# A linear-attention and SOLU feed-forward kernel on one core: the low mantissa bits of its weights made by another instruction on another engine, some copies moved to GpSimd, and a new order list

## The chip, the core and the metric

The kernel runs on one core of a Trainium2 chip. Five engines work side by side: TensorE (PE, with its weight loads shown apart as PEld), VectorE (DVE), ScalarE (ACT), GpSimd (POOL) and SyncE (SP), which issues all of this kernel's DMAs. Each engine takes its own instructions strictly in order. The metric is the device time of one execution in microseconds; the number compared is the median of several runs.

## What is computed

Eight batches, eight heads, 576 positions, head dimension 64. Linear attention gives 4608 rows of 512, and a feed-forward layer with a SOLU activation and a layer norm follows:

```python
q_s = softmax(q, axis=-1); k_s = softmax(k, axis=2)
kv = np.einsum('bhsd,bhse->bhde', k_s, v)
x = np.einsum('bhsd,bhde->bhse', q_s, kv)   # then turned to 4608 x 512
h = x @ w_in                                # 512 x 1024
solu = h * softmax(h)
ln = (solu - mean) / np.sqrt(var + 1e-06) * g_ln
return ln @ w_out                           # 1024 x 512
```

q, k, v and g_ln come as 4-byte floats. [...]

## The kernel before

The 4608 rows are 36 row tiles of 128. Works have short names: `K<b>` is the keys of batch b (column maxima, exponentials, the product with v, its scaled halves `bd`), `Q<b>a`, `Q<b>b`, `Q<b>c` and `R<b>` the queries, `V<b><i>` the load of a quarter of v and its copy into `vm` beside a column of ones, `x<t>` the attention product of row tiles from t on, `h<t>` the first matrix product of row tile t with everything up to the transposed activations `uT`, `o<t>` the second product and the store. `w<i>` and `y<i>` load and convert a quarter of w_in and of w_out, `W` and `Z` cut the converted weights into two half-precision parts `wi` and `wo` (part 0 is the value rounded to half precision, the "high half"; part 1 is the rest, the "low half"), and `P` is four products on zeros whose result nobody reads.

Every work is a generator. `ORDER` is a list, written out by hand, of steps: `step` advances the named work to its next yield, and a suffix `.v` sets `chosen`, so that `on(default)` returns VectorE in that step and the default engine otherwise. So the list fixes the order of the instructions on every engine, and no scheduler changes it.

**Converting the weights.** `float_of` (lines 251 to 264) takes a tile of words and makes the floats in three steps: ACT multiplies the high word, read as a float, into place (L259), DVE shifts the result's bits left by three (L261), and DVE shifts the low word right by 29 and puts its top three bits in (L263). Eight tiles of 128x1024 go through it, four `iw` and four `gw`. The words lie in a pool of two buffers, so the load of a tile waits until the words of the tile two before have been read. ACT then sums the absolute values of each converted tile (L276, L313); from the sums, by way of a product on PE (`wide_in`, `wide_out`), come the scales `s_in` and `s_out`, and from these `wi` (L288 on ACT, L290 on DVE, four tiles) and `wo` (L335 on ACT, L337 on DVE, eight pieces of 128x512).

**The first four row tiles.** They do not wait for `wi`: they multiply with `iw` itself at full 4-byte precision (L612, blocks in the order 3, 0, 2, 1). Their hidden values h lie in two PSUM buffers, so h of tile 2 starts when tile 0 has been read for the last time. In a tile the chain is: maximum on DVE (L627), its negative `nm` on ACT (L629), exponentials on ACT (L633), four small steps `am`, `pi`, `p`, `ph` on POOL or DVE (L637 to L646), the product on DVE (L649), the mean `nmu` on ACT (L651), `u` on ACT (L654), its rest on DVE (L656), the squares on ACT (L663). All later tiles multiply the half-precision parts (L620). The second product (L694) needs `wo` and `uT`.

The change and the prediction touch `float_of`, `load_v` (L212), `weights_in_scaled` (L288), `weights_out_scaled` (L335) and the list. In the changed kernel the code behind `float_of` stands eight lines lower (L620 is L628 there, L694 is L702).

## Time and profile before

| what | value |
|---|---|
| median of 3 runs | 464.75 us (463.77 to 465.03) |
| the profiled execution, its own time | 464.6 us |
| its span, first to last instruction | 462.8 us |
| PE busy | 439.2 us, 95% of the span |
| DVE, ACT, POOL busy | 339.3, 285.2, 202.6 us |
| mean granted TensorE clock | 0.999 |

The profiled execution's own time is 1.8 us longer than its span, and 0.15 us under the median. A busy PE is not a PE at its peak: durations of matmuls are modelled, and neighbours in a row overlap in the record, so that the start of the next row tells more than the duration. Idle time of PE is the quantity to follow.

### The profile page before, as it was taken

Reading aid. Unit: us, or ns where it says so; the run is one execution under the profiler, and the core shown is the slowest. Engines: PE = TensorE matmul, PEld = TensorE weight load, DVE = VectorE, ACT = ScalarE, POOL = GpSimd, SP = SyncE. Lnnn points to the kernel's source line nnn. Section 1 sums busy time; section 2 is a strip of 40 time slices with the busy share of each in tenths; the row PEclk is TensorE's granted clock in tenths of the full one; section 3 lists DMA queues with packets and bytes.
Section 4 is the critical chain, followed back from the end, with each engine's and each line's share of the span. In section 5 each row is a group of like instructions: output and inputs, shape, how many; then the busy total and the mean of one; then the engine's idle time right before and its main releaser. Section 6 shows DMA issues by size and latency. Waiting matters only on the chain.

```text
span 462.8 us, 8794 instructions
## 1 busy us (share of the span) xinstructions
PE 439.2 (95%) x3379; PEld 212.9 (46%) x3379; DVE 339.3 (73%) x622; ACT 285.2 (62%) x492; POOL 202.6 (44%) x308
## 2 busy tenths in 40 slices
PE   0688999999999999999999999999999999999997
PEld 0344444455445445444544445444454444444445
DVE  4989999987987979986987888675778553541711
ACT  2779998777767768385756674567635654441500
POOL 2112856487776664741455575126613421122010
PEclk9999999999999999999999999999999999999999
DMA  8897866788698496958697857774342562322252
GB/s 280 292 305 267 239 137 184 149 226 203 179 230 187 89 243 111 273 114 217 120 252 153 180 121 185 203 166 86 86 93 68 92 130 77 72 66 68 59 120 72
DMA packets 137386, 73.98 MB, mean 160 GB/s; under 512 B 114168, under 2 KB 122624, under 8 KB 137344
## 3 DMA queue, kind: packets, MB, share of 16 engines
q1 hardware_dynamic: 137344, 73.42, 65.1%
q8 instruction: 26, 0.43, 0.4%
q14 instruction: 16, 0.13, 0.1%
HBM read 36.70 MB, written 9.44 MB: 100 GB/s over the span
## 4 chain that ended last, share of the span: by engine, by line
PE 86%; ACT 7%; DVE 3%; DMA 1%; issue 1%; SPq 0%; ACTq 0%
PE o L694 41%; PE h L620 36%; PE kv L397 4%; PE x L585 3%; DMA km<-in_k_dram 1%; ACT gw L259 1%; ACT e L633 1%; PE h L612 1%; ACT km L385 1%; ACT wi L288 1%; ACT junk_out L313 1%; PE warm_up L751 1%; PE wide L358 1%; DVE iw L263 1%; ACT e L663 1%
## 5 line engine op out<-in xcount | busy, mean ns | idle before, releaser
L694 PE MATMUL o<-wo,uT 128*128 128x512 f16 (+1 forms) x888 | 197.8, 373 | 0.0
L620 PE MATMUL h<-wi,xT 128*128 128x512 f16 x768 | 178.0, 379 | 0.3 <-ACT e L663 0.3
L694 PEld LDWEIGHTS <-uT 128*128 128x128 f16 x888 | 85.8, 98 | 97.7 <-issue 1.6
L620 PEld LDWEIGHTS <-xT 128*128 128x128 f16 x768 | 74.3, 98 | 88.2 <-issue 1.8
L627 DVE TENSOR_REDUCE top<-h 128x1 f32<-128x1024 f32 x36 | 44.0, 1221 | 29.3 <-PE h L620 29.1
L656 DVE SCALAR_TENSOR_TENSOR u<-h,nmu,u 128x1024 f16<-128x1024 f32 x36 | 45.8, 1275 | 16.3 <-ACT u L654 16.1
L663 ACT ACTIVATE e<-h,nmu 128x1024 f32<-128x1024 f32 x36 | 40.1, 1113 | 21.2 <-DVE u L656 21.1
L649 DVE SCALAR_TENSOR_TENSOR h<-h,ph,e 128x1024 f32<-128x1024 f32 x36 | 46.1, 1283 | 8.1 <-POOL ph L646 6.1
L637 POOL TENSOR_SCALAR am<-nm 128x1 f32<-128x1 f32 x20 | 9.1, 454 | 80.7 <-ACT nm L629 80.6
L643 POOL TENSOR_TENSOR p<-pi,mone 128x1 f32<-128x1 f32 x36 | 25.5, 708 | 39.9 <-DVE pi L640 38.4
L654 ACT ACTIVATE u<-h,nmu 128x1024 f16<-128x1024 f32 x36 | 40.0, 1113 | 1.0
L633 ACT ACTIVATE e<-h,nm,hs 128x1024 f32<-128x1024 f32 x28 | 33.7, 1202 | 0.7
L704 ACT ACTIVATE os<-o,rr 128x512 f32<-128x512 f32 (+1 forms) x21 | 14.2, 674 | 30.2 <-PE o L694 22.9
L651 ACT ACTIVATE nmu<-s 128x1 f32<-128x1 f32 x36 | 7.3, 202 | 39.8 <-DVE h L649 31.9
L449 POOL TENSOR_TENSOR qm<-qm,qnmx 128x1024 f32<-128x1024 f32 (+1 forms) x12 | 21.1, 1770 | 20.6 <-DVE qnmx L447 20.5
L612 PE MATMUL h<-iw,xT 128*128 128x512 f32 x64 | 29.5, 599 | 0.1
L629 ACT ACTIVATE nm<-top,hs 128x1 f32<-128x1 f32 x28 | 8.2, 294 | 33.4 <-DVE top L627 33.4
L467 POOL TENSOR_TENSOR qm<-qm,qrec 128x1024 f32<-128x1024 f32 x12 | 23.0, 1920 | 11.7 <-DVE qrec L458 5.4
L383 POOL TENSOR_TENSOR km<-km,kb 128x1152 f32<-128x1152 f32 x10 | 26.3, 2632 | 3.4 <-ACT kb L361 3.2
L597 DVE SCALAR_TENSOR_TENSOR xT<-x,xT 128x512 f16<-128x512 f32 (+1 forms) x36 | 22.3, 623 | 7.2 <-ACT xT L595 7.1
L702 DVE TENSOR_SCALAR os<-o,rr 128x512 f32<-128x512 f32 (+1 forms) x16 | 11.6, 728 | 20.6 <-PE o L694 15.3
L474 POOL TENSOR_TENSOR qhl<-qm,qhl 128x512 f16<-128x512 f32 x20 | 24.1, 1228 | 5.3 <-ACT qhl L160 5.1
(147 smaller groups left out, 559.9 us busy)
## 6 DMA issues: line engine op xcount, KB each, us to landing
v<-in_v_dram SPq DMA_DIRECT2D x32, 288.0 KB, 3.9
km<-in_k_dram SPq DMA_DIRECT2D x7, 1152.0 KB, 6.4
out_dram<-os SPq DMA_DIRECT2D x31, 256.0 KB, 2.7
qm<-in_q_dram SPq DMA_DIRECT2D x7, 1024.0 KB, 6.7
w_in<-in_moe_w_in_dram SPq DMA_DIRECT2D x8, 512.0 KB, 8.4
w_out<-in_moe_w_out_dram SPq DMA_DIRECT2D x8, 512.0 KB, 5.8
out_dram<-os SPq DMA_DIRECT2D x10, 128.0 KB, 2.3
km<-in_k_dram SPq DMA_DIRECT2D x2, 576.0 KB, 6.8
```

Source lines behind the costliest of these rows:

```text
L383: on(nc.gpsimd).tensor_tensor(km[:, ns], km[:, ns], wide, op=ALU.subtract)
L474: on(nc.gpsimd).tensor_tensor(lo, y, hi, op=ALU.subtract)
L612: nc.tensor.matmul(h[:, ns], xT[:, kc], iw[kc][:, ns], start=(i == 0), stop=(i == NP - 1))
L620: nc.tensor.matmul(h[:, ns], xT[:, t, kc], wi[:, s, kc, ns], start=(i == 0), stop=(i == len(terms) - 1))
L627: nc.vector.tensor_reduce(top, h, axis=AX.X, op=ALU.max, negate=True)
L633: nc.scalar.activation(e, h, AF.Exp, bias=nm, scale=hs, accum_out=z)
L643: nc.gpsimd.tensor_tensor(p, pi, mone, op=ALU.pow)
L649: nc.vector.scalar_tensor_tensor(h, h, ph, e, op0=ALU.mult, op1=ALU.mult, accum_out=s1)
L654: nc.scalar.activation(u[:, 0], h, AF.Identity, bias=nmu)
L656: nc.vector.scalar_tensor_tensor(u[:, 1], h, nmu, u[:, 0], op0=ALU.add, op1=ALU.subtract)
L663: nc.scalar.activation(e, h, AF.Square, bias=nmu, accum_out=s2)
L694: nc.tensor.matmul(o, uT[:, j, f], wo[:, s, f, cols], start=(f == 0 and j == 0 and s == 0), stop=(f == NF - 1 and j == 1))
```

## The change

- `float_of` gets a step ahead of ACT's, which leaves the three bits as a small integer in the low word's place. In a step with `.v` DVE makes it (shift right by 29, a word in and a word out). In a step without, GpSimd makes it: it reads the low word's top byte as an unsigned 8-bit number, multiplies by 1/32, adds -31/64 and writes the rounded integer. What follows on DVE is one pass: shift the float's bits left by three and put the integer in. The pass that only shifted is gone.
- A new helper `scalar_or_pool` returns GpSimd in a step with `.v` and ACT otherwise. The copies of v use it in place of `on(nc.scalar)` (so `.v` there now means GpSimd, no longer DVE), and so do the high halves `wi` and `wo`, which were on ACT alone.
- `ORDER` is another list of the same works. It has nine `P` in place of eight.

```diff
+    def scalar_or_pool():
+        return nc.gpsimd if on(nc.scalar) is nc.vector else nc.scalar
...
-        cast(on(nc.scalar), vm[:, i, :, 0:D], t)
+        cast(scalar_or_pool(), vm[:, i, :, 0:D], t)
...
+        eng = on(nc.gpsimd)
+        if eng is nc.vector:
+            eng.tensor_scalar(low, low, 29, -1, op0=ALU.logical_shift_right, op1=ALU.bitwise_and)
+        else:
+            top = words.bitcast(U8)[:, :, 3]
+            eng.tensor_scalar(low, top, 1.0 / 32, -31.0 / 64, op0=ALU.mult, op1=ALU.add)
+        yield
         nc.scalar.activation(x, high.bitcast(F32), AF.Prelu, scale=2.0**-112, alpha=-(2.0**32))
         yield
-        nc.vector.tensor_scalar(xi, xi, 3, -1, op0=ALU.logical_shift_left, op1=ALU.bitwise_and)
-        yield
-        nc.vector.scalar_tensor_tensor(xi, low, 29, xi, op0=ALU.logical_shift_right, op1=ALU.bitwise_or)
+        nc.vector.scalar_tensor_tensor(xi, xi, 3, low, op0=ALU.logical_shift_left, op1=ALU.bitwise_or)
...
-            nc.scalar.activation(wi[:, 0, kc], iw[kc], AF.Copy, scale=s)
+            cast_scaled(scalar_or_pool(), wi[:, 0, kc], iw[kc], s)
...
-            nc.scalar.activation(wo[:, 0, f], x, AF.Copy, scale=g)
+            cast_scaled(scalar_or_pool(), wo[:, 0, f], x, g)
...
-    "LQ0*2 LK0 Q0a*2 Q0c LK0 K0.v Q0c.v K0 w3 K0.v K0 Q0b Q0a.v w3 K0 V02 Q0a Q0b K0.v Q0a.v Q0c V00 K0.v "
+    "LQ0*2 LK0*2 Q0a.v w3 Q0b.v Q0a Q0c V02.v P w3.v Q0b K0 K0.v Q0a K0*2 K0.v K0*2 V02.v Q0a V00.v w0.v "
```

Of the eight integer passes four are on DVE (`w_in` 3, 0, 1 and `w_out` 3) and four on POOL. Of the eight v copies of batches 0 and 1 seven are on POOL. Of the `wi` high halves one is on POOL, of the `wo` high halves two. Names in the order rows: the number behind a name tells one buffer from the next; `khalf`, `ktop` are the running maxima of the keys, `qm` and `km` the queries and keys of a batch, `qnmx`, `qsum`, `qden`, `qrec` the maxima and sums of the queries' softmax.

DVE at the start of the program, before:

```order
L449 TENSOR_TENSOR qm_95<-qm_95,qnmx_2_105 128x8x128
L374 TENSOR_TENSOR khalf_109<-khalf_109 128x2x128
L376 TENSOR_TENSOR ktop_108<-khalf_109 128x2x64
L377 TENSOR_TENSOR ktop_108<-ktop_108,km_98 128x2x64
L372 TENSOR_TENSOR khalf_109<-km_98 128x2x256
L447 TENSOR_REDUCE qnmx_1_118<-qm_95 128x8
L374 TENSOR_TENSOR khalf_109<-khalf_109 128x2x128
L454 TENSOR_REDUCE qsum_0_125<-qm_95 128x8
L456 TENSOR_SCALAR qden_0_127<-qsum_0_125 128x8
L458 RECIPROCAL qrec_0_129<-qden_0_127 128x8
L376 TENSOR_TENSOR ktop_108<-khalf_109 128x2x64
L377 TENSOR_TENSOR ktop_108<-ktop_108,km_98 128x2x64
```

and after:

```order
L455 TENSOR_REDUCE qnmx_2_110<-qm_95 128x16
L380 TENSOR_TENSOR khalf_122<-km_98 128x2x256
L382 TENSOR_TENSOR khalf_122<-khalf_122 128x2x128
L384 TENSOR_TENSOR ktop_121<-khalf_122 128x2x64
L385 TENSOR_TENSOR ktop_121<-ktop_121,km_98 128x2x64
L380 TENSOR_TENSOR khalf_122<-km_98 128x2x256
L382 TENSOR_TENSOR khalf_122<-khalf_122 128x2x128
L384 TENSOR_TENSOR ktop_121<-khalf_122 128x2x64
L385 TENSOR_TENSOR ktop_121<-ktop_121,km_98 128x2x64
L462 TENSOR_REDUCE qsum_0_136<-qm_95 128x8
L464 TENSOR_SCALAR qden_0_138<-qsum_0_136 128x8
L466 RECIPROCAL qrec_0_140<-qden_0_138 128x8
```

The key maxima `ktop` of batch 0 now stand together, ahead of the sums `qsum`; the addition into `qm` on DVE has gone further down. The first product on PE that needs data, the transpose of `ktop`, is released by the last of them.

POOL around the small steps of row tile 0 (`am`, `p`, `ph`), before:

```order
L464 TENSOR_TENSOR qn_2_104<-qm_95,qrec_2_289 128x2x4x64
L637 TENSOR_SCALAR am_0_450<-nm_0_431 128x1
L640 TENSOR_SCALAR pi_0_470<-am_0_450 128x1
L643 TENSOR_TENSOR p_0_473<-pi_0_470,mone 128x1
L646 TENSOR_TENSOR ph_0_475<-p_0_473,one 128x1
L383 TENSOR_TENSOR km_325<-km_325,kb_483 128x2x576
```

and after:

```order
L267 TENSOR_SCALAR w_in_205<-w_in_205 128x1024
L472 TENSOR_TENSOR qn_2_109<-qm_95,qrec_2_340 128x2x4x64
L267 TENSOR_SCALAR w_out_378<-w_out_378 128x1024
L168 COPY vm<-v_0_223 128x9x64
L645 TENSOR_SCALAR am_0_452<-nm_0_426 128x1
L267 TENSOR_SCALAR w_out_387<-w_out_387 128x1024
L651 TENSOR_TENSOR p_0_477<-pi_0_456,mone 128x1
L654 TENSOR_TENSOR ph_0_483<-p_0_477,one 128x1
L391 TENSOR_TENSOR km_347<-km_347,kb_490 128x2x576
```

Two integer passes on words of w_out and a copy of v now stand ahead of `ph`, on which row tile 0's product on DVE waits.

ACT around the exponentials `e` of row tile 0, before:

```order
L288 ACTIVATE wi<-iw_182,s_in 128x1024
L288 ACTIVATE wi<-iw_347,s_in 128x1024
L259 ACTIVATE gw_425<-w_out_397 128x1024
L426 ACTIVATE bd_80<-kvn_296,s_kv_358 64x256
L160 COPY vm<-v_2_395 128x9x64
L629 ACTIVATE nm_0_431<-top_0_429,one 128x1
L288 ACTIVATE wi<-iw_275,s_in 128x1024
L428 COPY bd_80<-bd_80 64x256
L259 ACTIVATE gw_445<-w_out_416 128x1024
L633 ACTIVATE e_0_447,z_0_448<-h_0_351,nm_0_431,one 128x1024
```

and after:

```order
L269 ACTIVATE gw_390<-w_out_378 128x1024
L637 ACTIVATE nm_0_426<-top_0_424,one 128x1
L641 ACTIVATE e_0_438,z_0_439<-h_0_370,nm_0_426,one 128x1024
L269 ACTIVATE gw_454<-w_out_387 128x1024
L172 ACTIVATE wi<-iw_202,s_in 128x1024
L434 ACTIVATE bd_80<-kvn_320,s_kv_368 64x256
L172 ACTIVATE xT_2_488<-x_2_0_465 128x256
L369 COPY kb_490<-wide_485 128x256
L436 COPY bd_80<-bd_80 64x256
L172 ACTIVATE wi<-iw_373,s_in 128x1024
```

The exponentials stood behind three high halves `wi`; now one conversion stands ahead of them and the first high half comes behind. A high half of the third block is no longer on ACT, and that of the last block comes only behind all `wo`, some forty rows further down.

## Rows read from the trace of the kernel before

**Rows 1.** The page's parts 1 and 2: busy time with share of the span and instruction count of each engine, then the busy tenths of 40 slices of 11.6 us.

```profile
PE 439.2 (95%) x3379; PEld 212.9 (46%) x3379; DVE 339.3 (73%) x622; ACT 285.2 (62%) x492; POOL 202.6 (44%) x308
...
DVE  4989999987987979986987888675778553541711
ACT  2779998777767768385756674567635654441500
POOL 2112856487776664741455575126613421122010
```

**Rows 2.** The windows view of core 0 for the stretch before 72.5 us and the stretch behind it; columns: stretch, its length, busy time (and instructions) of PE, PEld, DVE, ACT, POOL, granted TensorE clock as a share of full speed, DMA share, GB/s.

```profile
0.00:72.50 72.50, 52.34 (x493) 26.49 (x494) 62.25 (x120) 57.99 (x96) 26.01 (x33) 1.00 0.79 244
72.50:463.00 390.50, 386.90 (x2886) 186.41 (x2885) 277.08 (x503) 227.25 (x397) 176.56 (x276) 1.00 0.63 144
```

**Rows 3.** The waits view of PE over the whole span; columns: who waited for whom, us in total, times, longest.

```profile
PE turned L348 <- DVE ktop L377: 14.3, 1, 14.3
PE wide L358 <- ACT cols L160: 2.2, 2, 1.5
PE kv L397 <- ACT km L385: 1.1, 1, 1.1
...
PE h L620 <- ACT e L663: 0.3, 1, 0.3
```

**Rows 4.** The timeline of PE from 0 to 120 us; columns: start, duration (both us), engine, line, operation, out<-in, shape, count, and in brackets the idle time before it with its releaser.

```profile
14.29 0.66 PE L348 MATMUL turned<-ident,ktop 128*128 128x128 f32 x2 [14.29 <-DVE ktop L377]
...
17.23 1.91 PE L751 MATMUL warm_up<-bd 128*128 128x512 f16 x4
...
22.38 1.89 PE L751 MATMUL warm_up<-bd 128*128 128x512 f16 x4
24.19 1.58 PE L397 MATMUL kv<-vm,km 64*64 64x65 f32 x72
...
26.20 1.03 PE L751 MATMUL warm_up<-bd 128*128 128x512 f16 x4
...
34.30 3.60 PE L612 MATMUL h<-iw,xT 128*128 128x512 f32 x8
...
51.25 7.03 PE L612 MATMUL h<-iw,xT 128*128 128x512 f32 x16
...
72.53 1.89 PE L620 MATMUL h<-wi,xT 128*128 128x512 f16 x8 [0.27 <-ACT e L663]
74.25 1.46 PE L694 MATMUL o<-wo,uT 128*128 128x512 f16 x6
```

**Rows 5.** The timeline of DVE from 0 to 90 us, same columns.

```profile
8.76 1.22 DVE L449 TENSOR_TENSOR qm<-qm,qnmx 128x1024 f32<-128x1024 f32 x1
...
12.41 0.68 DVE L454 TENSOR_REDUCE qsum<-qm 128x8 f32<-128x512 f32 x1
...
13.85 0.29 DVE L377 TENSOR_TENSOR ktop<-ktop,km 128x128 f32<-128x128 f32 x1
...
26.70 1.39 DVE L261 TENSOR_SCALAR iw<-iw 128x1024 int32<-128x1024 int32 x1
...
31.43 1.23 DVE L263 SCALAR_TENSOR_TENSOR iw<-w_in,iw 128x1024 int32<-128x1024 int32 x1
...
38.17 1.22 DVE L627 TENSOR_REDUCE top<-h 128x1 f32<-128x1024 f32 x1
...
45.73 1.29 DVE L649 SCALAR_TENSOR_TENSOR h<-h,ph,e 128x1024 f32<-128x1024 f32 x1
...
68.71 0.23 DVE L330 TENSOR_SCALAR gs<-gl,s_out 128x8 f32<-128x8 f32 x1
```

**Rows 6.** The timeline of ACT from 0 to 90 us, same columns.

```profile
40.16 0.29 ACT L629 ACTIVATE nm<-top,one 128x1 f32<-128x1 f32 x1
...
43.00 1.19 ACT L633 ACTIVATE e<-h,nm,one 128x1024 f32<-128x1024 f32 x1
...
49.87 1.11 ACT L663 ACTIVATE e<-h,nmu 128x1024 f32<-128x1024 f32 x1
...
65.20 1.08 ACT L313 ACTIVATE junk_out<-gw 128x1024 f32<-128x1024 f32 x1
...
71.28 1.10 ACT L663 ACTIVATE e<-h,nmu 128x1024 f32<-128x1024 f32 x1
```

**Rows 7.** Groups of DVE instructions by line, shapes kept apart, over the whole span; columns: line, engine, operation, out<-in, shapes, count, busy us, mean ns of one, idle before.

```profile
L263 DVE SCALAR_TENSOR_TENSOR gw<-w_out,gw 128x1024 int32<-128x1024 int32 x4 | 4.9, 1222 | 0.0
...
L261 DVE TENSOR_SCALAR gw<-gw 128x1024 int32<-128x1024 int32 x4 | 2.7, 684 | 0.0
```

**Rows 8.** Groups of ACT instructions by line, shapes kept apart, of the stretch 0 to 72.5 us, same columns.

```profile
L160 ACT COPY vm<-v 128x576 f32<-128x576 f32 x8 | 5.3, 668 | 0.0
...
L288 ACT ACTIVATE wi<-iw,s_in 128x1024 f16<-128x1024 f32 x4 | 4.5, 1138 | 0.0
```

**Rows 9.** Groups of POOL instructions by line, shapes kept apart, over the whole span, same columns.

```profile
L449 POOL TENSOR_TENSOR qm<-qm,qnmx 128x1024 f32<-128x1024 f32 x10 | 18.9, 1904 | 11.6 <-DVE qnmx L447 11.5
...
L449 POOL TENSOR_TENSOR qm<-qm,qnmx 128x512 f32<-128x512 f32 x2 | 2.2, 1098 | 9.0 <-DVE qnmx L447 9.0
...
L143 POOL MEMSET bd<- 128x1024 f16 x1 | 1.0, 952 | 0.3 <-POOLq L800 0.3
```

**Rows 10.** The timeline of POOL from 0 to 120 us, columns as in the other timelines.

```profile
26.49 1.05 POOL L464 TENSOR_TENSOR qn<-qm,qrec 128x512 f32<-128x512 f32 x1 [2.52 <-PE qt L519]
```

More of the change, by code (lines that the diff above doesn't have):

```diff
@@ L13 @@
 I32 = mybir.dt.int32
+U8 = mybir.dt.uint8
 AF = mybir.ActivationFunctionType
```

145 rows, old and new, of the table ORDER are left out of this document.

## The prediction

> **What bounds the kernel now.** I read the busy shares first, then where PE is idle, then the chain that ends PE's idle time. PE is busy for 95% of the span, DVE, the next, for 73% [rows 1]. So the question is what PE's idle time is made of. The windows say that it lies at the two ends: up to 72.5 us PE is busy for 52.3 us, so 20.2 are idle, and in the 390.5 behind that only 3.6 are [rows 2]. Of these 3.6 a wait of 0.3 is the only one; the rest follows the last product. The waits of PE agree: 14.3 us until the first transpose of the keys' maxima, some small ones, and 0.3 for the squares of a row tile [rows 3], which is the wait in front of the row at 72.53 [rows 4]. From there on PE works without a gap.
>
> So the kernel's time is a start plus a constant: 72.53, then 390.3 to the end of the span (462.8), then 1.8 outside the span, 464.6 for the profiled execution; the median of the runs is 464.75. The work of PE behind 72.53 is the same in both kernels (the same products, and the warm-ups all lie ahead), so whatever the change does off PE there costs nothing as long as PE does not run dry. What can move the time is the start.
>
> In the start DVE is busy for 62.3 us of 72.5 and ACT for 58.0, POOL for 26.0 [rows 2]; from the third to the seventh slice DVE is at 8 or 9 tenths or more and ACT at 7 to 9 [rows 1]. PE fills its time there with products whose result nobody reads. Two chains cross: weights (words, float, sum, scale, halves) and the first four row tiles, each of which passes DVE and ACT eight times and holds one of two PSUM buffers meanwhile.
>
> **What the change takes away and adds.** Up to the scales of w_out, ACT loses seven of eight v copies at 0.668 and two of four `wi` high halves at 1.138 [rows 8]: 4.7 + 2.3 = 7.0 us. DVE loses four of eight passes at 0.684 [rows 7], 2.7 us, and takes over half of the subtraction on batch 1's keys, 1152 elements, about 1.4 by L263's pace (1.222 for 1024 [rows 7]): net 1.3 less. Only half of the "second pass" really leaves DVE; the other half stays as a pass on the words. POOL gets four byte passes, seven copies, one high half. Nothing like them is in the trace, so they are bounded: for 1024 elements 0.95, the memset that only writes, to 1.90, the two-input sum; for 576 elements 0.54 to 1.24, by the same two rows and the 512-element one scaled [rows 9]. All together 8.5 to 18 us; POOL goes from 26 to some 35 to 44 of 72.5, so it is not full, but what stands behind a late piece waits. I take 1.3 for a byte pass, between the ends since it reads one stream and writes one. None of these can be below nothing: they are added instructions. The cost of the two `wo` high halves on POOL lies behind the scales, beside DVE's low halves.
>
> The DVE pass on words with a gap between them is not in the trace either: the same operation on dense data takes 0.684, a pass at one element a cycle 1.222 [rows 7]. I take 0.95, the middle; each then costs 0.27 over the dense one, 0.8 for the three on w_in; the fourth, on w_out, I take as hidden beside ACT's sums.
>
> The Trainium skill, "VectorE: DVE Perf Modes", section "What auto-detection actually checks", gives the double rate to one source and a destination in SBUF whose outermost dimension is even, as 1024 is, whatever the gap. By it the pass takes 0.684 and the time comes out 0.8 us lower, 461.6; no row here shows the gapped pass.
>
> **The path, checkpoint by checkpoint** (before, then after).
>
> 1. First transpose of the maxima: 14.29 [rows 4]. On DVE the 1.22 of the addition at 8.76 and the sums from 12.41 to the last maximum but one (13.85 less 12.41, less one 0.27 step, 1.2) stood between the maxima [rows 5]; both now come behind. 14.29 - 2.4 = 11.9, or 14.29 if the second part of the keys lands late; I take 12.3. Only part of this is carried on, since the exponentials of the keys also wait for DVE.
>
> 2. End of row tile 0's full-precision products: 34.30 + 3.60 = 37.9 [rows 4]. The last conversion they need ended at 31.43 + 1.23 = 32.7 [rows 5]. Off DVE ahead of it are now the pass of 1.39 at 26.70 (now POOL's) and the last block's own pass, which runs beside ACT's: 2.0 less, 30.6. Behind it one block, half of 3.60, and two transposes, and the wait for `wide_in` stands behind: 33.5. Gain 4.4.
>
> 3. Product of row tile 0 on DVE: 45.73 [rows 5]. The maximum (38.17 [rows 5]) comes behind batch 1's key maxima at 34.5, the exponentials then follow `nm` at once (before: 40.16 to 43.00 [rows 6], behind high halves). But DVE has two conversions, a low half (1.28, as the other two-source passes) and the scale chain to do in between: 34.5 + 1.2 + 1.2 + 1.2 + 1.3 and 2.1 of small steps = 41.5. Gain 4.2.
>
> 4. End of its squares, which frees the buffer for row tile 2: 49.87 + 1.11 = 51.0 [rows 6]. Now an exponential of the keys and that of row tile 1 (1.19) stand ahead of the squares: gain 3.1, 47.9; row tile 2's products on PE (51.25 before [rows 4]) follow at once.
>
> 5. Last sum of w_out: 65.20 + 1.08 = 66.3 [rows 6], and the scales 68.71 [rows 5]. Row tiles 1 and 2 carry the gain of the buffer on: 63.2 and 65.7.
>
> 6. Start of the gapless stretch: 72.53 [rows 4]. It now begins with the second product, which before came second at 74.25 [rows 4]. It needs two low halves of `wo` behind the scales and a rest of `u` on DVE, 65.7 + 0.2 + 1.3 + 1.5 = 68.7, and PE has the last blocks of row tile 3 to finish, 69.1. Raw gain 3.4.
>
> From this I take off 0.8 for the gapped DVE passes and 0.4 for two-source passes that meet a POOL instruction (below). 70.3 + 390.3 + 1.8 = **462.4 us**, 2.2 less than the profiled execution.
>
> TensorE's clock is granted at full (2.4 GHz) throughout in the record [rows 2], yet four warm-up products took 1.91 and 1.89 at first and 1.03 from 26.20 [rows 4]. The list now starts them ahead of the first transpose. At the slow pace the products on batch 0's keys end about where I have them, at the fast one 1 us earlier; since row tile 0 waits for its weights, I count nothing.
>
> **Rivals.** *DVE alone sets the start.* With DVE nearly full, ACT's 7 us are worth nothing and only DVE's own 1.3 less count, minus the 1.2 taken off: 464.5, with 463.4 to 465.2 around it. For it: the digits of DVE [rows 1]. Against it: the rows of ACT ahead of the exponentials (2.8 us from `nm` to `e`) are on the path.
>
> *POOL and DVE block each other*, the one that ends slower. The DVE pass at 26.70 took 1.39, where its like take 0.684 [rows 5, 7], and POOL's instruction from 26.49 to 27.54 lies over it [rows 10]: 0.7 us lost in one meeting. The change adds twelve POOL instructions ahead of the scales, and DVE has some twenty passes there with two operands in SBUF. Eight meetings would take 5.6 of a raw gain of 3.4: 466.8. From five on the gain is gone. A late byte pass does the same by another way, since `ph` stands behind two of them.
>
> The Trainium skill, "SBUF — State Buffer", section "Who interferes with whom", has this as a rule: a DVE instruction in a two-port mode, or one with two SBUF inputs against a GpSimd instruction that reads SBUF, and that instruction exclude each other for their whole length. By that rule this rival's price holds for every meeting; the trace agrees, 1.39 against 0.684. It leaves open how many meet.
>
> *PE runs dry later.* The last `wi` block's high half now comes behind all of `wo` on ACT, and its low half behind row tile 3's product on DVE. I work out its end at 79.5, and PE wants it 11.2 us into the gapless stretch, about 81. If the chain is 3 us late, PE waits 1.5 or more: 464.
>
> **How the numbers follow.** The forecast with its own range 460.4 to 463.3: 0.60. DVE alone: 0.22. PE dry later: 0.05. Blocking: 0.13. The range for 8 in 10 takes in all but the last and the edges: 459.9 (gapped passes at the double rate, no meeting, the clock 1 us earlier) to 465.2. A difference under 0.3%, 1.4 us, can't be told from none: faster 0.60 (the forecast), same 0.27 (DVE alone and PE dry, 463.4 to 466.1), slower 0.13 (blocking).
>
> **What would show it.** Right: PE's first transpose near 12.3, row tile 0's squares ending near 48, the scales near 66, the gapless stretch starting near 70.3 and no wait of PE behind it. DVE alone: the early checkpoints move, the scales stay above 68. Blocking: conversions on DVE (L271) well over 1.25 us in the mean. The forecast is wrong if a byte pass takes over 2 us, or if PE waits after 71.

## The result, and the profile after

The changed kernel is slower: 466.84 us in the median of 12 runs (465.54 to 468.91) against 464.45 us of 12 runs of the kernel before (463.77 to 465.89) on the same chip, a ratio of 1.0057 with a 95% interval of 1.0044 to 1.0071. The forecast was 462.4. Executions of the changed kernel lie up to 3.4 us apart, those of the kernel before 2.1; so a single profile is read below for order and for the length of single instructions, and times are compared by medians.

The profiled execution took 467.61 us, with a span of 465.8. TensorE (PE), its waits and its first and last steps of the start, as in [rows 4]:

```profile
12.45 0.66 PE L356 MATMUL turned<-ident,ktop 128*128 128x128 f32 x2 [8.84 <-DVE ktop L385]
...
33.29 3.60 PE L620 MATMUL h<-iw,xT 128*128 128x512 f32 x8
...
51.75 8.83 PE L620 MATMUL h<-iw,xT 128*128 128x512 f32 x16 [2.43 <-ACT e L671]
...
74.75 2.75 PE L702 MATMUL o<-wo,uT 128*128 128x512 f16 x12
```

The first transpose comes 1.84 us earlier than in [rows 4], as forecast. Of that, 1.0 is left when row tile 0's products end (33.29 + 3.60 = 36.9), and the gapless stretch starts 2.2 us later than before. VectorE (DVE) on the way, to be held against the same forms in [rows 5, 7]:

```profile
17.55 1.84 DVE L391 TENSOR_TENSOR km<-km,kb 128x1152 f32<-128x1152 f32 x1
...
20.38 1.34 DVE L391 TENSOR_TENSOR km<-km,kb 128x1152 f32<-128x1152 f32 x1
...
22.78 2.16 DVE L457 TENSOR_TENSOR qm<-qm,qnmx 128x1024 f32<-128x1024 f32 x1
...
41.67 1.22 DVE L168 COPY cols<-col 128x256 f32<-128x256 f32 x1
...
45.30 1.29 DVE L657 SCALAR_TENSOR_TENSOR h<-h,ph,e 128x1024 f32<-128x1024 f32 x1
...
68.09 1.29 DVE L657 SCALAR_TENSOR_TENSOR h<-h,ph,e 128x1024 f32<-128x1024 f32 x1 [0.28 <-POOL ph L654]
...
72.01 0.23 DVE L338 TENSOR_SCALAR gs<-gl,s_out 128x8 f32<-128x8 f32 x1
```

Two passes of one form, on keys of the same size, took 1.84 and 1.34; the addition L457 took 2.16 where it took 1.22 in [rows 5]. What lay beside them stands in the timeline of GpSimd (POOL):

```profile
17.42 2.49 POOL L168 COPY vm<-v 128x576 f32<-128x576 f32 x2 [2.28 <-DMA v<-in_v_dram]
22.46 1.43 POOL L267 TENSOR_SCALAR w_in<-w_in 128x1024 int32<-128x1024 uint8 x1 [2.55 <-PE kv L405]
...
39.43 1.72 POOL L168 COPY vm<-v 128x576 f32<-128x576 f32 x1
...
41.64 1.10 POOL L267 TENSOR_SCALAR w_out<-w_out 128x1024 int32<-128x1024 uint8 x1
42.83 1.63 POOL L651 TENSOR_TENSOR p<-pi,mone 128x1 f32<-128x1 f32 x1
...
61.85 2.85 POOL L174 TENSOR_SCALAR wi<-iw,s_in 128x1024 f16<-128x1024 f32 x1
64.79 1.34 POOL L648 TENSOR_SCALAR pi<-am 128x1 f32<-128x1 f32 x1
66.21 1.58 POOL L651 TENSOR_TENSOR p<-pi,mone 128x1 f32<-128x1 f32 x1
```

(The 8-byte weights are read as pairs of 4-byte words; a byte pass takes the top byte of the low words.) The v copies overlap the pass of 1.84 us and the byte pass that of 2.16. And the small steps of a row tile (`am`, `pi`, `p`, `ph`) stand behind the new pieces in one order: `p` of row tile 0 behind a copy and a byte pass, `pi` of row tile 2 behind a scaled high half of 2.85 us.

### The profile page after: what moved, and what is told of

Its sections match the earlier page's. It is cut to its first block, busy times and chain, and to the rows that moved or that the text cites. A ratio compares the mean times of both kernels' runs of the same rounds, so it can differ in the third digit from the quotient of the medians.

```text
span 465.8 us, 8819 instructions
## 1 busy us (share of the span) xinstructions
PE 441.8 (95%) x3383; PEld 213.0 (46%) x3383; DVE 342.2 (73%) x617; ACT 277.5 (60%) x474; POOL 221.2 (47%) x331
## 4 chain that ended last, share of the span: by engine, by line
PE 83%; DVE 4%; DMA 4%; ACT 3%; POOL 3%; issue 1%; SPq 0%; ACTq 0%; DVEq 0%; POOLq 0%
PE o L702 40%; PE h L628 36%; PE x L593 3%; PE kv L405 3%; DMA w_out<-in_moe_w_out_dram 2%; DMA w_in<-in_moe_w_in_dram 1%; DMA qm<-in_q_dram 1%; DVE h L657 1%; DVE iw L271 1%; POOL p L651 1%; POOL wi L174 1%; POOL qhl L482 1%; DVE qnmx L455 1%; DVE w_in L264 0%; ACT km L393 0%
## 5 line engine op out<-in xcount | busy, mean ns | idle before, releaser
L648 POOL TENSOR_SCALAR pi<-am 128x1 f32<-128x1 f32 x27 | 8.5, 314 | 68.3 <-DVE am L645 65.4
L712 ACT ACTIVATE os<-o,rr 128x512 f32<-128x512 f32 (+1 forms) x19 | 12.8, 671 | 34.4 <-PE o L702 25.2
L620 PE MATMUL h<-iw,xT 128*128 128x512 f32 x64 | 30.8, 628 | 2.4 <-ACT e L671 2.4
L645 POOL TENSOR_SCALAR am<-nm 128x1 f32<-128x1 f32 x23 | 7.8, 341 | 52.8 <-ACT nm L637 52.4
L684 POOL TENSOR_TENSOR r<-var,mhalf 128x1 f32<-128x1 f32 x36 | 21.3, 591 | 21.9 <-DVE var L681 21.1
L475 POOL TENSOR_TENSOR qm<-qm,qrec 128x1024 f32<-128x1024 f32 x12 | 23.7, 1972 | 12.3 <-DVE qrec L466 5.8
L710 DVE TENSOR_SCALAR os<-o,rr 128x512 f32<-128x512 f32 (+1 forms) x18 | 13.2, 733 | 21.8 <-PE o L702 10.1
```

Source lines behind the costliest of these rows:

```text
L475: on(nc.gpsimd).tensor_tensor(x, x, wide(rec), op=ALU.mult)
L620: nc.tensor.matmul(h[:, ns], xT[:, kc], iw[kc][:, ns], start=(i == 0), stop=(i == NP - 1))
```

## Experiments

Each was timed against the kernel before on the same chip, whose median was 464.2 to 464.7 us in every group; the changed kernel stands at 1.0057. The ratios come from runs side by side and are not quotients of these medians. The tail of e9_pairs was looked at once and not timed.

| run | what differs | median, us | ratio to the kernel before, 95% |
|---|---|---|---|
| e1_old_list | new code, old list | 473.98 | 1.0219 (1.0188 to 1.0250) |
| e4_low_dve | byte passes to VectorE | 473.21 | 1.0181 (1.0155 to 1.0207) |
| e2_halves_act | high halves to ScalarE | 469.39 | 1.0106 (1.0087 to 1.0126) |
| e3_v_act | v copies to ScalarE | 467.11 | 1.0051 (1.0031 to 1.0070) |
| e5_piece_later | one high half later | 470.92 | 1.0127 (1.0104 to 1.0151) |
| e6_later_v_act | e5 and e3 | 472.21 | 1.0148 (1.0117 to 1.0178) |
| e10_low_later | high half later, low half behind gs | 468.42 | 1.0079 (1.0059 to 1.0099) |
| e8_words3 | last w_in words elsewhere | 466.22 | 1.0034 (1.0016 to 1.0052) |
| e11_low_later_words | e10 and e8 | 465.81 | 1.0042 (1.0024 to 1.0059) |
| e13_before_words | kernel before with e8's edit | 464.93 | 1.0004 (0.9993 to 1.0015) |
| e7_warm | three more idle groups on PE | 466.94 | 1.0059 (1.0038 to 1.0081) |
| e14_no_bytes | no byte passes | 466.20 | 1.0049 (1.0021 to 1.0077) |
| e15_no_v | no v copies on GpSimd | 464.34 | 0.9999 (0.9975 to 1.0024) |
| e16_no_both | neither | 461.94 | 0.9960 (0.9938 to 0.9982) |
| e17_no_three | neither, and no high halves | 460.79 | 0.9923 (0.9897 to 0.9949) |
| e18_fills | fills in place of passes and copies | 465.56 | 1.0027 (1.0012 to 1.0041) |
| e19_before_v_direct | kernel before, v loaded into vm | 464.64 | 0.9994 (0.9980 to 1.0009) |

**One part of the change alone.** The new code under the old list, and the changed kernel with its byte passes moved to VectorE:

```
-ORDER = (the new list)
+ORDER = (the list of the kernel before)
```

Expected of e1_old_list:

> The changed code with the list of the kernel before: no scaled high half stands on GpSimd any more, the byte pass of all eight weight tiles is on GpSimd, and the v copies that the list marks too. List theory (the new order itself placed the work worse): the time comes back to that of the kernel before or below it, 462.5 to 464.8 us. Blocking theory (each piece moved to GpSimd lengthens VectorE's passes beside it): still over the kernel before, 465.5 to 467. Queue theory (large pieces stand ahead of am, pi, p and ph in GpSimd's order): the byte passes wait for words in that queue, the wi and wo pieces are gone, so 464 to 465.5.

```
-        eng = on(nc.gpsimd)
+        eng = nc.vector
```

Expected of e4_low_dve:

> The changed kernel with every low pass on VectorE (the strided pass of 0.68 us), none from the byte on GpSimd. Blocking theory: the byte passes of 1.1 us each no longer hold VectorE, against 0.68 us for each one that VectorE now does: within 0.5 us of the changed kernel, 466.3 to 467.2. Queue theory: the byte passes no longer wait for words at the head of GpSimd's queue, 465.5 to 466.3. If the byte pass was worth what it was made for (VectorE's time), 467.5 to 469.

Both lost 6 to 7 us more. The waits of GpSimd in the first and of VectorE in the second, over the span (who waited for whom, us in total, times, longest):

```profile
POOL w_in L266 <- DMA w_in<-in_moe_w_in_dram: 10.1, 2, 8.3
POOL w_out L266 <- DMA w_out<-in_moe_w_out_dram: 6.4, 2, 5.8
```

```profile
DVE w_out L264 <- DMA w_out<-in_moe_w_out_dram: 4.0, 1, 4.0
```

A pass on freshly loaded words holds whatever is behind it until they land, on either engine: `qn`, on which PE then waited 2.2 us, in the first, the sums of w_in in the second (PE waited 2.7). So these two tell of places in a list, not of the pieces' price. The first shows that the old list fits the new code worse (under it all eight byte passes are on GpSimd); whether the new list costs something is told only by the pieces left out, below.

**One kind of piece back on ScalarE.**

```
-            cast_scaled(scalar_or_pool(), wi[:, 0, kc], iw[kc], s)
+            cast_scaled(nc.scalar, wi[:, 0, kc], iw[kc], s)
...
-            cast_scaled(scalar_or_pool(), wo[:, 0, f], x, g)
+            cast_scaled(nc.scalar, wo[:, 0, f], x, g)
```

Expected of e2_halves_act:

> The changed kernel with all high halves of w_in and w_out on ScalarE, nothing else changed. Queue theory: the piece of 2.85 us ahead of pi in row tile 2 is gone and gs comes about 3 us earlier, so 463.5 to 464.5 us. Blocking theory: only the passes beside these three pieces get shorter (about 0.5 us in all), so 466 to 466.6. List theory: no difference, 466.4 to 467.2; ScalarE has up to 3.4 us more work in the prologue, which could take the gain back.

```
-        cast(scalar_or_pool(), vm[:, i, :, 0:D], t)
+        cast(nc.scalar if b < 2 else scalar_or_pool(), vm[:, i, :, 0:D], t)
```

Expected of e3_v_act:

> The changed kernel with the v copies of batches 0 and 1 back on ScalarE. Blocking theory: the VectorE passes that ran beside them (1.84 for 1.34, 2.16 for 1.22, 1.22 for 0.29 us and others) are short again, about 2 us of the start come back, 464.5 to 465.3 us. Queue theory: about 1 us, am and p of row tile 0 no longer wait for the copies, 465.5 to 466.2. List theory: no difference, 466.4 to 467.2.

All three theories were off for the first: 2.5 us slower. In its profile ScalarE's high half stands behind a sum of w_out, VectorE's low half waits 1.50 us for it, and the sum of the last w_out tile begins at 68.55 instead of 67.45. But `gs` comes only 0.5 us later than in the changed kernel (72.53), and the gapless stretch 2.9 later (77.68): behind a wait of PE for the sum of w_out the granted clock fell to 0.65 in 70 to 75 us, and PE's last products ahead of the stretch took 3.78 for 1.98. The second left the time as it was, though row tile 2's products began 1.1 us earlier and `gs` came at 70.83, 1.2 earlier; 0.8 of that went again in the same way (stretch at 74.41). So the two runs do not show that ScalarE has no room for the pieces; part of what they measure is PE's clock.

**Moving what stands in the way.** In the list, with steps counted from 0, `W.v` numbers 8 and 9 are the third high half of w_in and its low half; `h2` number 9 is `ph`, number 10 the product of row tile 2; `Z` number 3 makes `gs`.

```
-... h2.v y2 W.v K1 y1 h2.v h2 h3.v K1.v h2.v K1 W.v ... y3*2 h2 K1 ...
+... h2.v y2 K1 y1 h2.v h2 h3.v K1.v h2.v K1 ... y3*2 h2 W.v W.v K1 ...
```

Expected of e5_piece_later:

> The changed kernel with one piece moved in the list: the high half of the third tile of w_in on GpSimd, and the low half that follows it on VectorE, come behind ph of row tile 2 instead of ahead of pi. Queue theory (that piece of 2.85 us and the wait of VectorE's low half for it hold pi, the conversion of the last w_out tile and so gs): gs comes 2.5 to 3 us earlier, and the time is 463.8 to 464.6 us. Blocking theory (the passes themselves are longer wherever both engines work): the piece blocks as much in its new place, 466.2 to 467. Theory of the late words (w_in and w_out words land as late as ever): something else is late next and gives less than 1 us, 465.8 to 466.6.

Expected of e6_later_v_act:

> The move of the run before it together with the v copies of batches 0 and 1 on ScalarE. With the copies on ScalarE alone the products of row tile 2 began 1.1 us earlier and ended 2.8 us earlier, and the high half ahead of pi ended only 1.2 us earlier. Queue theory: with the piece gone from there the earlier products count, 462 to 463.5 us. Blocking theory: 464.5 to 465.5, from the copies alone. If the last words of w_out are what sets gs, no more than the move alone gives.

Every theory missed. VectorE in the first of them, around row tile 2's product:

```profile
66.51 2.91 DVE L301 SCALAR_TENSOR_TENSOR wi<-iw,s_in,wi 128x1024 f16<-128x1024 f32 x1 [0.72 <-POOL wi L177]
...
69.79 1.27 DVE L660 SCALAR_TENSOR_TENSOR h<-h,ph,e 128x1024 f32<-128x1024 f32 x1
```

The low half, 1.28 us where it met nobody, now met a GpSimd addition of 1.90 us that reads two tensors, took 2.91, and stood ahead of the product. `gs` came 1.6 and 1.3 us later than in the changed kernel (73.65 and 73.35); some 2 us more were lost behind it, where PE was granted 0.57 of its clock in 70 to 78 us (the stretch began at 78.37 and 77.87). The next edit puts the low half behind `gs`:

```
-... y3*2 h2 W.v W.v K1 ...  Z.v h2.v ...
+... y3*2 h2 W.v K1 ...  Z.v W.v h2.v ...
```

Expected of e10_low_later:

> The changed kernel with the high half of the third w_in tile on GpSimd behind ph of row tile 2, and its low half on VectorE behind gs. In the run where the low half stood ahead of row tile 2's product it waited 0.72 us for GpSimd and then took 2.91 us beside another GpSimd pass, and the product began at 69.8 us although ph was there at 63.6. Queue theory: now the product begins near 66, gs comes near 70 instead of 72, TensorE's gapless stretch begins near 72.5, and the time is 464.3 to 465.2 us. Blocking theory: the passes of the chain lose again what the order gives, 466 or more.

```
+        if name == "in1":
+            w = (wo[:, 0] as 1024 pairs of 32-bit words)
```

Expected of e8_words3:

> The changed kernel with the words of the last w_in tile loaded into the space of wo, which nothing uses before 72 us, so that they need not wait until the conversion of another tile frees a buffer (they were issued at 22.9 us, when VectorE had finished that conversion). If VectorE's lengthened passes, through that buffer, are why row tile 0's full-precision products ended at 36.9 us and not at 33.5: the words land 2 to 4 us earlier, those products end at 34 to 35.5, and the time is 465 to 466 (or less, if the later stages follow in full: 463.5). If the DMA engines are the limit there: the words land at most 1 us earlier and the time stays at 466.4 to 467.2, or other words land later for it.

Expected of e11_low_later_words:

> That order together with the words of the last w_in tile in the space of wo, which alone began TensorE's gapless stretch at 72.0 us in its profiled run (74.75 in the changed kernel) and gave 466.2 us as the median. If both delays are on one path and add: the stretch begins at 69.5 to 70.5 us and the time is 462 to 463.5, below the kernel before. If they do not add: 464 to 466.

Expected of e13_before_words:

> The kernel before, with nothing of the change, and the words of the last w_in tile in the space of wo. If the wait for that buffer costs the kernel before as much as the changed one: 462.5 to 464 us. If there the words wait for the DMA engines or for their place in the list: within 0.5 us of the kernel before. It shows whether the gain of that edit has anything to do with the change.

The queue theory's number for the single move failed: gs came at 72.38, not near 70. The conversion of the last w_out tile took 1.92 beside the moved high half, and VectorE came to it late because PE's transpose of `mx` stood behind products that waited for squares. After `gs`, the low half took its 1.28 us there, GpSimd's first high half of w_out took 2.51 beside it, and PE waited 0.4 us twice. (In this execution PE had also waited 2.6 us for the last words of w_in.) The words' place gave the changed kernel at most 0.2 per cent, the intervals overlapping, and the kernel before nothing; with the move on top it is no better (1.0042 and 1.0034). So in these runs no single wait set the start.

```
-P K1 h0 y3.v ...
+P P P K1 h0 y3.v ...   (and one P ahead of the turning of m_out)
```

Expected of e7_warm:

> The changed kernel with three more idle groups of four products on TensorE, nothing else: two ahead of row tile 2's products (where it waited 2.4 us for the squares) and one ahead of the turning of the weights' largest sums (where it waited 2.0 us). If the lowered clock behind such waits is part of the loss (row tile 2's products took 8.83 us at 0.91 granted in 40 to 60 us, 7.03 in the kernel before): granted clock 1.00 in every stretch, row tile 2's products 7.1 us, and 465 to 466 us, with less spread from run to run. If the stage is set by GpSimd and VectorE anyway: 466.4 to 467.2.

In the changed kernel PE, idle for 2.43 us ahead of row tile 2's products, was granted 0.91 in 40 to 60 us, a mix of 2.4 and 1.2 GHz. Here it was 1.00 in every stretch of the profile, and those products took 7.13 us instead of 8.83 (in e5, behind a wait as long, they took 7.13 too, so the wait alone does not decide it):

```profile
49.31 7.13 PE L623 MATMUL h<-iw,xT 128*128 128x512 f32 x16 [0.25 <-ACT e L674]
```

The median stayed at 1.0059: the lowered clock in this stretch of the start cost nothing that could be measured, and the executions still lie as far apart (465.40 to 468.83). It is otherwise where the clock falls just ahead of the gapless stretch, as in e2 and e15 (below).

**The pieces in pairs.**

```
+        for d in (*range(4), None):      # VectorE's pieces, or none
+            for g in (*range(4), None):  # GpSimd's pieces, or none
+                together(d, g)
```

Expected of e9_pairs:

> The changed kernel with a tail of pieces measured alone and in pairs after its last store: on VectorE the combining pass with two sources, the strided pass, the maximum along a row and the widening copy of 256; on GpSimd the copy of 576, the byte pass, the scaled copy to 16 bits and the power of one column. Nothing of the kernel itself is changed; the time grows by the tail, some 150 to 250 us. Blocking theory: in some pairs a piece takes 1.5 times as long or more as alone, on either engine, above all the strided pass, the widening copy and the power beside GpSimd's copies; the maximum along a row leaves GpSimd alone. Without blocking: every piece takes beside the other engine what it takes alone, within 5%.

The tail took VectorE and GpSimd through all pairs; a row holds four instructions (eight of the widening copy and of the power), and after each group both engines meet. The timeline of VectorE: the combining pass beside copies, byte passes, scaled copies, powers and nothing; the strided pass beside copies, byte passes and nothing; the maximum beside byte passes and nothing; the widening copy beside byte passes and nothing.

```profile
469.54 6.02 DVE L808 SCALAR_TENSOR_TENSOR pa<-pb,pwv 128x1024 int32<-128x1024 int32 x4
...
476.98 7.27 DVE L808 SCALAR_TENSOR_TENSOR pa<-pb,pwv 128x1024 int32<-128x1024 int32 x4
...
486.21 6.43 DVE L808 SCALAR_TENSOR_TENSOR pa<-pb,pwv 128x1024 int32<-128x1024 int32 x4
...
499.92 5.00 DVE L808 SCALAR_TENSOR_TENSOR pa<-pb,pwv 128x1024 int32<-128x1024 int32 x4
...
508.74 4.99 DVE L808 SCALAR_TENSOR_TENSOR pa<-pb,pwv 128x1024 int32<-128x1024 int32 x4
...
514.63 3.89 DVE L809 TENSOR_SCALAR pwv<-pwv 128x1024 int32<-128x1024 int32 x4
...
519.95 5.17 DVE L809 TENSOR_SCALAR pwv<-pwv 128x1024 int32<-128x1024 int32 x4
...
548.20 2.88 DVE L809 TENSOR_SCALAR pwv<-pwv 128x1024 int32<-128x1024 int32 x4
...
557.86 4.97 DVE L810 TENSOR_REDUCE p<-pb 128x1 f32<-128x1024 f32 x4
...
582.17 4.97 DVE L810 TENSOR_REDUCE p<-pb 128x1 f32<-128x1024 f32 x4
...
593.07 5.95 DVE L811 COPY pa<-pb 128x256 f32<-128x256 f32 x8
...
618.39 2.58 DVE L811 COPY pa<-pb 128x256 f32<-128x256 f32 x8
```

GpSimd: the copies and the powers beside the combining pass, then the four pieces alone.

```profile
469.54 6.54 POOL L814 COPY pga<-pgb 128x576 f32<-128x576 f32 x4
...
500.13 7.68 POOL L817 TENSOR_TENSOR p<-p,mone 128x1 f32<-128x1 f32 x8
...
621.97 2.84 POOL L814 COPY pga<-pgb 128x576 f32<-128x576 f32 x4
...
625.92 4.59 POOL L815 TENSOR_SCALAR pwp<-pwp 128x1024 int32<-128x1024 uint8 x4
...
631.64 11.32 POOL L816 TENSOR_SCALAR pgh<-pgb 128x1024 f16<-128x1024 f32 x4
...
644.09 4.96 POOL L817 TENSOR_TENSOR p<-p,mone 128x1 f32<-128x1 f32 x8
```

Blocking holds, in this measure: the four copies add 1.0 us to VectorE's combining passes (6.02 against 4.99, 0.26 each), the four byte passes 2.3 (7.27 against 4.99, 0.57 each); the strided pass loses the same (1.0 and 2.3), and the widening copy beside byte passes takes 5.95 for 2.58. The maximum loses nothing. GpSimd pays as well: a copy takes 1.64 instead of 0.71. A byte pass that is there to spare VectorE a pass of 0.72 gives 0.57 of it back when it meets such passes. And the scaled copy to 16 bits takes 2.83 us alone, without anyone in its way; ScalarE's takes 1.14 [rows 8].

The Trainium skill, "SBUF — State Buffer", section "Who interferes with whom", names the same forms: two-port passes, and passes with two inputs against GpSimd's reads, but not a maximum along a row. The pairs agree (4.97 and 4.97 for the maximum, 7.27 against 4.99 for two inputs). They do not agree that the instructions exclude each other for their whole length, as the prediction has it: beside byte passes both rows together took 8.22 us, where 4.99 and 4.59 one after the other would be 9.58, and beside copies 6.54 where 4.99 and 2.84 would be 7.83.

**The pieces left out.** What GpSimd got from the change is taken away kind by kind, everything else kept, the list and ScalarE's and VectorE's relief too. With a piece go the waits for its result, and without the v copies VectorE fills `vm` with a constant at the start.

```
-            eng.tensor_scalar(low, top, 1.0 / 32, -31.0 / 64, op0=ALU.mult, op1=ALU.add)
+            low = zero.broadcast_to([P, DF])
```

Expected of e14_no_bytes:

> The changed kernel without its byte passes on GpSimd: for these four weight tiles the low bits are left out and VectorE's combining pass reads a zero in their place, so the weights lose their lowest bits; everything else stands as it was. If the byte passes cost what the pairs measured (0.57 us of VectorE each) and what their waits in GpSimd's order hold up: 1.5 to 3 us less, 463.8 to 465.3. If they hide: within 0.6 us of the changed kernel.

```
+        if b > 1 or scalar_or_pool() is nc.scalar:
             cast(scalar_or_pool(), vm[:, i, :, 0:D], t)
```

Expected of e15_no_v:

> The changed kernel without the v copies of batches 0 and 1 that stand on GpSimd: they are left out and vm holds ones there, so the sums over the values are not those of v. If they cost VectorE 0.26 us each and GpSimd's order 0.7 to 1.7 us each: 1 to 2.5 us less, 464.3 to 465.8. If the move to ScalarE gained nothing because nothing of them is on the path: within 0.6 us of the changed kernel.

Expected of e16_no_both:

> Byte passes and v copies both left out. If GpSimd's added pieces are why the forecast failed: near the forecast's 462.4 us, the gapless stretch from 70 to 71. If the start is set by the words' landing and the chain of the other engines: 465 or more, the stretch from 73 on.

```
+            if scalar_or_pool() is nc.scalar:
                 cast_scaled(nc.scalar, wi[:, 0, kc], iw[kc], s)
```

Expected of e17_no_three:

> As the run before it, and the scaled high halves of w_in and w_out that stand on GpSimd are left out too (zeros in the place of w_in's). This is all that the change puts on GpSimd ahead of the gapless stretch, made free. Theory that GpSimd's pieces cost the gain: 461.5 to 463 us, the stretch from 69.5 to 71. Theory of list and landing: no lower than 464.5, although GpSimd is no busier than in the kernel before.

This settles that the loss is GpSimd's pieces. Without the copies the time falls by 2.5 us, without the byte passes too by 4.9, and without the high halves too by 6.05 (466.84 to 460.79). Without the byte passes alone it falls by 0.6, which is not clear of noise, and neither is the step from 461.94 to 460.79, as the intervals overlap. PE's clock also took part of what leaving out the copies gave: in the profiled execution (465.1 us) `gs` came 4.8 us earlier than in the changed kernel (67.21), but the gapless stretch only 2.6 earlier (72.16), with 0.61 and 0.54 granted in 66 to 70 and 70 to 74 us. PE ahead of the stretch there, and in the changed kernel, which was granted 1.00 in 65 to 75 us:

```profile
65.46 0.29 PE L178 MATMUL wide_out<-ident,m_out 128*128 128x128 f32 x1 [2.32 <-DVE m_out L332]
...
68.58 3.78 PE L621 MATMUL h<-iw,xT 128*128 128x512 f32 x4
```

```profile
72.93 1.98 PE L620 MATMUL h<-iw,xT 128*128 128x512 f32 x4
```

So how much each kind costs by itself is open. PE and VectorE in the last of the four runs:

```profile
12.80 0.66 PE L360 MATMUL turned<-ident,ktop 128*128 128x128 f32 x2 [9.18 <-DVE ktop L389]
...
30.88 3.60 PE L624 MATMUL h<-iw,xT 128*128 128x512 f32 x8
...
69.55 2.75 PE L706 MATMUL o<-wo,uT 128*128 128x512 f16 x12
```

```profile
37.88 0.28 DVE L171 COPY cols<-col 128x256 f32<-128x256 f32 x1
...
41.13 1.28 DVE L661 SCALAR_TENSOR_TENSOR h<-h,ph,e 128x1024 f32<-128x1024 f32 x1
...
66.62 0.23 DVE L342 TENSOR_SCALAR gs<-gl,s_out 128x8 f32<-128x8 f32 x1
```

VectorE's fill of `vm`, which the changed kernel lacks (there it fills the column of ones alone, in 0.09 us), in a time when VectorE otherwise waits for the first loads:

```profile
1.40 2.01 DVE L145 MEMSET vm<- 128x2340 f32 x1 [0.46 <-issue]
```

The widening copy takes 0.28 us, 1.22 in the changed kernel. The windows up to `gs`, of the changed kernel and of this run (columns as in [rows 2]):

```profile
0.00:72.20 72.20, 51.85 (x481) 25.44 (x481) 60.54 (x111) 49.60 (x81) 43.64 (x44) 0.98 0.79 246
```

```profile
0.00:66.90 66.90, 51.33 (x481) 25.66 (x481) 57.74 (x112) 49.40 (x81) 27.82 (x33) 0.97 0.84 265
```

VectorE is busy for 60.54 us in one and, without the fill, for 57.74 - 2.01 = 55.73 in the other, and from 5 us on it makes the same 107 instructions in both. So 4.8 us of the 5.3 by which the window is longer are passes made longer: the addition L457 and the widening copy by nearly 1 us each, the strided passes on w_in by 0.7 together, the rest by less. Some 4 of the 4.8 lie beside the new copies and byte passes. VectorE's waits account for the other 0.5.

**By which way.**

```
-            eng.tensor_scalar(low, top, 1.0 / 32, -31.0 / 64, op0=ALU.mult, op1=ALU.add)
+            eng.memset(low, 0)
...
+            nc.gpsimd.memset(vm[:, i, :, 0:D], 1.0)
```

Expected of e18_fills:

> The changed kernel with each of GpSimd's four byte passes and seven v copies of batches 0 and 1 replaced by a fill of the same elements (zeros for the low bits, ones for v; the low bits of four weight tiles and the values of v are left out), in the same place of GpSimd's order. A fill reads nothing. Blocking theory: VectorE's passes beside the fills keep their own length (the additions on the keys 1.34 us, the widening copy 0.3, the strided pass 0.7), and the time is near that without the pieces, 462 to 463.5 us. Queue theory: the fills hold am, p and qn as long as the pieces did, 465.5 to 467. If a fill blocks VectorE as well, the passes stay long and nothing is told apart.

The time fell between the two numbers: 1.3 us of the 4.9 come back. VectorE beside the fills:

```profile
14.21 1.33 DVE L467 TENSOR_SCALAR qden<-qsum 128x8 f32<-128x8 f32 x1
...
22.73 1.22 DVE L460 TENSOR_TENSOR qm<-qm,qnmx 128x1024 f32<-128x1024 f32 x1
...
49.59 1.65 DVE L267 TENSOR_SCALAR w_out<-w_out 128x1024 int32<-128x1024 int32 x1
```

The addition that took 2.16 beside a byte pass takes 1.22 beside a fill: passes with two inputs are no longer held. But `qden` takes 1.33 instead of 0.3 and the strided pass 1.65 instead of 0.7. So a fill still lengthens these passes with one input, and the run doesn't separate blocking from order: from 5 us up to `gs`, which comes 1.9 us later than in e17, VectorE's passes are 3.1 us longer than there. The 4.8 and 0.5 us of the windows are the nearest to a split that the runs give.

```
+        if b < 2:
+            nc.sync.dma_start(out=vm[:, i, :, 0:D], in_=src)
+            yield
+            return
```

Expected of e19_before_v_direct:

> The kernel before, with none of the change, and v of batches 0 and 1 loaded straight into vm (rows of 256 bytes in place of 2304), so that no engine copies it: ScalarE loses eight copies of 0.668 us. If ScalarE's copies are on the path of the start: 462 to 464 us. If the many small rows slow the loads, which keep the DMA engines at nine tenths up to 40 us: 465 to 470. If neither matters: within 0.5 us of the kernel before.

No gain that can be measured (0.9980 to 1.0009). Its profiled execution began the gapless stretch at 70.78, 1.75 us earlier than in [rows 4], while the median over 12 runs is that of the kernel before; the DMA engines were at 0.99 and 1.05 of their time in the first two slices of 20 us. What takes the gain back in the other executions stays open. No run beats the kernel before with the whole computation done.

## Why the prediction was wrong, point by point

The forecast took 390.3 + 1.8 behind the start of the gapless stretch; measured 391.05 + 1.8, a wait of 0.16 among it. The start is where it failed:

| checkpoint, us | before | forecast | changed | pieces left out (e17) |
|---|---|---|---|---|
| first transpose | 14.29 | 12.3 | 12.45 | 12.80 |
| end of row tile 0's products | 37.9 | 33.5 | 36.9 | 34.5 |
| product of row tile 0 on VectorE | 45.73 | 41.5 | 45.30 | 41.13 |
| end of row tile 0's squares | 51.0 | 47.9 | 51.6 | 47.5 |
| scales `gs` | 68.71 | 65.7 | 72.01 | 66.62 |
| gapless stretch | 72.53 | 70.3 | 74.75 | 69.55 |

1. *The first transpose* was right: nothing of the change on GpSimd stands ahead of it.

2. *The relief of VectorE and ScalarE, and the list* were right. With GpSimd's pieces made free, the checkpoints come out at the forecast's, within 1 us, and the time at 460.79. The forecast without its allowance for meetings (0.4) and for the strided pass (0.8) is 461.2. (The lower end of its range, 459.9, does not follow from the three terms that it names: 462.4 less 0.8, 0.4 and 1 is 460.2.)

3. *The term that failed* is "0.4 for two-source passes that meet a POOL instruction", with POOL "not full". VectorE's passes up to `gs` were 4.8 us longer for the pieces (60.5 against 55.7), and the pieces cost 6.05 us in all. GpSimd's busy time grew as forecast (43.6 us up to `gs`, 35 to 44 expected), the lengths of pieces were right where they met nobody (byte pass 1.1 us for 1.3 taken, copy 0.66 to 0.71; the scaled half, in 6, was not). The number of meetings was the error: VectorE was busy for 60.5 of the 72.2 us, so that a new piece should meet a pass more often than not (argued; the meetings were not counted), and in the pairs each meeting costs both engines. A row that showed one such meeting at 0.7 us [rows 5, 10] was used for a small allowance instead of being multiplied.

4. *The second checkpoint* shows it first. The forecast carried 4.4 us of gain to row tile 0; the changed kernel had 1.0. Behind the v copies of batch 0 and a byte pass, VectorE's passes from 17.5 to 25 us are 1.9 us longer than without the copies (17.55, 19.31 and 22.78 us against their forms), PE waited 1.2 us for `vm`, and the last words of w_in were issued at 22.9 when VectorE had freed their buffer. Without the copies the second half of these products began at 30.6 instead of 33.3.

5. *The strided pass* was priced at 0.95; unblocked it takes 0.68 to 0.72, so the 0.8 taken off was too much, and in the changed kernel blocking put part of it back (0.98 and 1.15 for two of four). "VectorE: DVE Perf Modes" of the Trainium skill, section "What auto-detection actually checks", gave the double rate; the runs agree with 0.68.

6. *The scaled high half on GpSimd* was put within its busy time, at no more than 1.90 us; at 2.85 it is above that bound and 2.5 times ScalarE's 1.14 [rows 8], and it stands ahead of `pi` and of VectorE's low half. What it costs by itself is open: taking it away as well gave 1.15 us (461.94 to 460.79), not clear of noise, and moving it gave nothing.

7. *Rivals.* "POOL and DVE block each other" came out, at its time (466.8), and its 5.6 us lost on VectorE were near the 4.8 that the windows give. That it hit the time within 0.1 us is in part luck: it has eight meetings at 0.7, while in the pairs a meeting with a copy or a byte pass costs a combining pass 0.26 to 0.57, and VectorE's waits are in no term of it. Blocking's sign for the profile, conversions well over 1.25 us in the mean, was weak: L271 on w_in had 1.22, on w_out 1.30; the lengthened passes were others. "DVE alone sets the start" (464.5) had the scales stay above 68, and they did (72.01); but with the pieces left out and VectorE's own instructions kept they come at 66.62 and the time at 460.79, so this rival does not hold. "PE runs dry later" did not happen.

8. *The clock.* It reached full pace by 16 us, earlier than before, and fell to 0.91 in 40 to 60 us behind a wait of PE; in the run with more idle products, whose profile has 1.00 throughout, the time was the same, so counting nothing for it was right for the changed kernel. In other runs it was not nothing: from `gs` to the gapless stretch the changed kernel takes 2.74 us at a granted clock of 1.00; in the profiles of e15 and e2 it takes 4.95 and 5.15, at 0.54 and 0.69 in 70 to 74 us.

## What to carry to other kernels

An engine with idle time is not free if its instructions lengthen those of the busiest one (here four combining passes took 7.27 us instead of 4.99 beside byte passes): multiply the price of one meeting by the number of pieces, since beside an engine that is busy for 84% of the time (60.5 of 72.2 us) most pieces can be expected to meet something. Price a piece by its effect on both engines' chains; here a byte pass that spares VectorE 0.72 us takes 0.57 back in a meeting, and the pieces as a whole cost 6 us for a relief worth 3.6. Leaving pieces out kind by kind told the cause, where moving them one at a time had told little. And hold what such a run puts in their place against the other instruction by instruction: here a fill of 2.0 us at the start hides two fifths of what VectorE's passes gained, and in one profile a lowered clock of PE hides nearly half of what leaving out the copies gave.

## What the runs showed of the hardware that was not expected

A fill on GpSimd, which only writes, left VectorE's two-input addition at 1.22 us but stretched a strided one-input pass from 0.68 to 1.65 and a pass over eight columns from 0.3 to 1.33. Eight powers of one column each took 4.96 us alone and 7.68 beside four combining passes of 1.25, while those passes lost nothing (5.00 against 4.99): the small steps of the chain are held by VectorE far more than they hold it. A scaled copy from 32 to 16 bits takes GpSimd 2.83 us for 1024 columns, the byte pass over as many 1.15.
